# Where attention output is turned token by token: in the feed-forward stage instead of the gradient phase

## The chip, the cores and the metric

The kernel runs on one core of one Trainium2 chip. The metric is the device time of one execution in microseconds (us), and the time of a kernel is the median of several runs. The kernel computes the forward and the backward pass of one transformer block in a single launch.

In the profile PE is the engine that does matrix products and transposes, DVE, ACT and POOL do elementwise work, and SP only issues DMAs. SPq and POOLq rows are DMA issues on the instruction streams of SP and POOL; each stream runs strictly in order, and a DMA whose data or buffer isn't ready holds up everything behind it on that stream.

## The reference

The block is an attention part that runs over 64 segments one after another, with 8 memory tokens carried from segment to segment, and a SwiGLU feed-forward part. All tensors are bf16; S = 2048 tokens, D = 448, 16 heads of 256 (4096 columns, HD), F = 1792.

```python
h  = x + A(layernorm(x))          # A: segments of 32 tokens + 8 memory tokens
h2 = h + B(layernorm(h))          # B: (silu(x @ w_gate) * (x @ w_up)) @ w_down

# A, for each segment s, hcat = concat(mem, xs):
q, k, v = hcat @ Wq, hcat @ Wk, hcat @ Wv
p = softmax(where(mask, q @ k.T * scale, -1e9))
o = (p @ v) @ Wo
mem = o[:8]; out_s = o[8:]

out, vjp = jax.vjp(f, A_x, A_mem0, A_Wq, A_Wk, A_Wv, A_Wo, w_gate, w_up, w_down)
return out, *vjp(grad_out)
```

So ten outputs: the block's output and nine gradients. The gradient of Wo is a product of `p @ v` (called O here, all 4096 columns of it) with the gradient that reaches the attention output, summed over all tokens, and the gradients of Wq, Wk and Wv are products of the normed input with dQ, dK and dV.

## The kernel before

The program has four stages, in this order.

**Forward chain** (`forward_chain`). 64 segments in sequence; four segments make one tile of 128 token rows, t = 0 to 15. For each tile it keeps O in feature-major form, `oA` (128 features by 32 chunks by 128 tokens), and when the fourth segment of the tile is done POOL stores it to the DRAM tensor `OTA[t]`, 1 MB each. The eight memory tokens of each segment go to `OTB`.

**Feed-forward stage** (`ffn_phase`, with buffers that `_FFN` cuts out of the large SBUF tensor `Wall`, whose quarters W[0] to W[3] hold weights). A loop `for i in range(NT - 2)` goes over the tiles. Each iteration handles several tiles at once: the gradient `dz` and the output of tile t, the gate and up products of the next tile n1, the norm of the one after, n2. What it does on the two DMA streams, in program order, with the line that issues it:

- SP: `load(n2)` (L1055, L1057, L1058) loads the rows of `Hh` and of grad_out of tile n2. Its buffer `h_ld` has three slots, and the slot becomes free when `down_ev` (L1149) of tile t-1 has read it. The data is needed by `norm(n2)` (L1063), late in the same iteration.
- POOL: `DH` and `DHb` of tile t-1 (L1179, L1182), `DGP` and `DU` of tile t (L1158, L1161), `doutT` (L1198), the block's output (L1150), `HN` (L1066), `Zt` of tile n1 (L1116). The buffers `dh_t` (of `DH`), `dgp` and `du` have one slot each, so DVE can write the next tile's values only when the store of this one has landed. `z` has two.
- In iteration i = 2 there is also `load_back` of the transposed Wo: four DMA transposes on SP (L1016, L1017) and a memset on POOL (L1018), which overwrites rows that the last of them has written and therefore waits for it.

**Backward chain** (`backward_chain`): the 64 segments in reverse, which store dQ, dK and dV feature-major as `dQA`, `dKA`, `dVA`, in the same form as `OTA`.

**Gradient phase** (`tail_phase`). It has 22 pieces, p = 0 to 21. Pieces 0 to 5 are feed-forward weight gradients. Pieces 6 to 21 are the four quarters (1024 of 4096 columns) each of v, k, q and o, in this order. Each piece is one run of matrix products over all tokens (L1864 and L1877 for v, k and q; L1849 for o) with a 5 MB operand X, which holds tokens in the partitions. There are three X buffers, so X of piece p+2 takes the buffer of piece p-1; `load_phase(p + 2)` is written at the start of piece p. As the stored tensors are feature-major, `seg_x` turns them while loading: 16 DMA transposes on SP (L1804), one for each tile, of 128 by 1024 values (256 KB). The rows of the memory-adjacent tokens come by another way: `seg_b_load` (POOL, L1813), a POOL copy (L1819), PE transposes (L1826). Also on SP in every piece from 5 on are three loads for the last layernorm (L1888 to L1892) and, from 6 on, a store of the result (L1904); in piece 8 there are the loads of the 2 MB operand of the o pieces (L1796 to L1799).

The change touches `_FFN`, the loop of `ffn_phase`, and `seg`, `srcA` and `load_phase` of `tail_phase`.

Of the kernel before, what the change touches and what calls it, by code (L numbers as in the profile page):

```python
# [10 lines left out]
BF16 = mybir.dt.bfloat16  # L11
# [4 lines left out]
P = 128  # L16


class _Prio:

    def __init__(self, tc):
        self.tc = tc
        self.next = -50_000_000
# [242 lines left out]
def run_all(k: _K):  # L266
    nc, tc, ctx = k.nc, k.tc, k.ctx
    S, D, M, H, Dh, HD, F = k.S, k.D, k.M, k.H, k.Dh, k.HD, k.F
    SEG, L, NSEG, NT, KC, DP, MC, DC, FC = k.SEG, k.L, k.NSEG, k.NT, k.KC, k.DP, k.MC, k.DC, k.FC
# [12 lines left out]
    dram = ctx.enter_context(tc.tile_pool(name="dram", bufs=1, space=bass.MemoryType.DRAM))  # L282
# [13 lines left out]
    def ps3(n=3):  # L296
# [32 lines left out]
    Vtok = dram.tile([NSEG, 2, 48, HD // 2], BF16, name="Vtok")  # L329
    OTA = dram.tile([NT, P, MC * P], BF16, name="OTA")  # L330
    OTB = dram.tile([NT, P, MC * SEG], BF16, name="OTB")
    DHb = dram.tile([S, D], BF16, name="DHb")
    dxnTd = dram.tile([NT, P, KC * P], FP32, name="dxnTd")
    memTd = dram.tile([P, KC, NSEG * M], BF16, name="memTd")
    dmemTd = dram.tile([P, KC, NSEG * M], BF16, name="dmemTd")
    memtok = dram.tile([NSEG * M, D], BF16, name="memtok")
    dmemtok = dram.tile([NSEG * M, D], BF16, name="dmemtok")
    dQA = dram.tile([NT, P, MC * P], BF16, name="dQA")
    dKA = dram.tile([NT, P, MC * P], BF16, name="dKA")
    dVA = dram.tile([NT, P, MC * P], BF16, name="dVA")  # L340
    dQB = dram.tile([NT, P, MC * SEG], BF16, name="dQB")
    dKB = dram.tile([NT, P, MC * SEG], BF16, name="dKB")
    dVB = dram.tile([NT, P, MC * SEG], BF16, name="dVB")
    doutTd = dram.tile([NT, P, KC * P], BF16, name="doutTd")
    P_all = dram.tile([NSEG, 64 + L, H // 2 * 64], BF16, name="P_all")
    dr = dict(XN=XN, Hh=Hh, HN=HN, DH=DH, Zt=Zt, DGP=DGP, DU=DU, QtokA=QtokA, KtokA=KtokA, QtokB=QtokB, KtokB=KtokB, Vtok=Vtok,
              OTA=OTA, OTB=OTB, DHb=DHb, dxnT=dxnTd, memT=memTd, dmemT=dmemTd, memtok=memtok, dmemtok=dmemtok, dQA=dQA, dKA=dKA, dVA=dVA, dQB=dQB, dKB=dKB, dVB=dVB, doutT=doutTd, P_all=P_all)
    k.dr = dr

    wts = ExitStack()  # L350
# [3 lines left out]
    W = [k.Wall[:, i * WS:(i + 1) * WS] for i in range(4)]  # L354
    ff = _FFN(k, W)
# [26 lines left out]
    with tc.manual_schedule():  # L382
# [25 lines left out]
        Xs = W[3][:, 0:NT * D].rearrange("p (t d) -> p t d", t=NT)  # L408
# [72 lines left out]
def forward_chain(k: _K, hA, NWIN, Wq_sb, Wk_sb, Wv_sb, Wo_sb, maskr, work, stage, ff, feed):  # L481
# [290 lines left out]
    for s in range(NSEG):  # L772
# [172 lines left out]
        if r == 3:  # L945
            nc.gpsimd.dma_start(out=dr["OTA"][t], in_=T.oA[:].rearrange("p c n -> p (c n)"))
            nc.gpsimd.dma_start(out=dr["OTB"][t], in_=T.oB[:].rearrange("p c n -> p (c n)"))
        late2 = late
# [15 lines left out]
class _FFN:  # L964

    def __init__(self, k, W):
        self.k = k
        P_, F, D, KC, FC = P, k.F, k.D, k.KC, k.FC
        n1 = KC * F
        n2 = FC * D  # L970
        self.Wg = W[0][:, 0:n1].rearrange("p (c f) -> p c f", c=KC)
        self.Wu = W[0][:, n1:2 * n1].rearrange("p (c f) -> p c f", c=KC)
        self.Wd = W[1][:, n1:n1 + n2].rearrange("p (c d) -> p c d", c=FC)
        self.zT = W[1][:, n1 + n2:n1 + n2 + F].rearrange("p (c n) -> p c n", c=FC)
        self.WgT = W[2][:, 0:n2].rearrange("p (c d) -> p c d", c=FC)
        self.WuT = W[2][:, n2:2 * n2].rearrange("p (c d) -> p c d", c=FC)
        self.dgpT = W[2][:, 2 * n2:2 * n2 + F].rearrange("p (c n) -> p c n", c=FC)
        self.duT = W[2][:, 2 * n2 + F:2 * n2 + 2 * F].rearrange("p (c n) -> p c n", c=FC)

    def load_first(self):  # L980
        k, nc = self.k, self.k.nc
        D = k.D
        full = D // P
        rem = D - full * P
        for dst, src, eng in ((self.Wg, k.aps["B_w_gate"], nc.gpsimd), (self.Wu, k.aps["B_w_up"], nc.gpsimd)):
            eng.dma_start(out=dst[:, 0:full, :], in_=src[0:full * P, :].rearrange("(kc p) n -> p kc n", p=P))
            for h in range(2):
                eng.dma_start(out=dst[rem * h:rem * (h + 1), full, :], in_=src[full * P:D, :])
# [21 lines left out]
def load_back(k, v, src, head, c0=0, c1=None):  # L1010
    nc = k.nc
    D, HD = k.D, k.HD
    if head:
        full = D // P
        for kc in range(full):
            nc.sync.dma_start_transpose(out=v[:, kc, :], in_=src[:, kc * P:(kc + 1) * P])  # L1016
        nc.sync.dma_start_transpose(out=v[:, full, :], in_=src[:, D - P:D])  # L1017
        nc.gpsimd.memset(v[0:P - (D - full * P), full, :], 0.0)  # L1018
    else:
        nc.sync.dma_start_transpose(out=v[:, c0:c1, :], in_=src[:, c0 * P:c1 * P])  # L1020


def ffn_phase(k: _K, WT, ff, work, mv2, rstd2, srcs, back):
    nc, tc = k.nc, k.tc
    S, D, F = k.S, k.D, k.F
    NT, KC, DP, FC = k.NT, k.KC, k.DP, k.FC
    ps1, ident, dr = k.ps1, k.ident, k.dr
# [21 lines left out]
    def rows(t):  # L1049
        return slice(t * P, (t + 1) * P)  # L1050

    def load(t):
        o = T[t]
        o.h = work.tile([P, D], BF16, name="h_ld", bufs=3)
        nc.sync.dma_start(out=o.h[:], in_=dr["Hh"][rows(t), :])  # L1055
        o.dout = work.tile([P, DP], BF16, name="dout_ld", bufs=4)
        nc.sync.dma_start(out=o.dout[:, 0:D], in_=GO2[rows(t), :])  # L1057
        nc.sync.dma_start(out=o.dout[:, D:DP], in_=GO2[rows(t), D - rem:D])  # L1058
# [125 lines left out]
    def dh_out(t):  # L1184
# [12 lines left out]
        A(dT[:], pt[:, 0:KC * P])  # L1197
        nc.gpsimd.dma_start(out=dr["doutT"][t], in_=dT[:])  # L1198

    sd = smal.tile([P, NT], FP32, name="sd2")  # L1200

    def rstd(a, b):
# [30 lines left out]
    for i in range(NT - 2):  # L1233
        t, n1, n2 = ORD[i:i + 3]
        if i > 0:
            load(n2)
        if i == 2:
            load_back(k, WT["o"], srcs["o"], True)
        if i == NT - 6:
            next(back)  # L1240
        turn_f(T[t].z, ff.zT, (A, A))
        dz(t)
        if i > 0:
            dh_ln(t - 1)
        down_mm(t)
        if i == 0:
            rstd(NT - 1, NT)
        grads(t)
        if i > 0:
            dh_out(t - 1)  # L1250
        gate(n1)
        down_ev(t)
        norm(n2)
        up(n1)
        if i == NT - 3:
            dout_turn(n1)
            hn_turn(n2)
            gate(n2)
            load_back(k, WT["v"], srcs["v"], False, 0, HC)
            up(n2)  # L1260
            load_back(k, WT["v"], srcs["v"], False, HC, 2 * HC)
            dh_turn(t)
            slope(n1)
            slope(n2)
        else:
            dh_turn(t)
            dout_turn(n1)
            hn_turn(n2)
            slope(n1)
        dh_mm(t)  # L1270
    p, q = ORD[NT - 2:]
# [483 lines left out]
def tail_phase(k: _K, work):  # L1755
    nc, tc = k.nc, k.tc
    S, D, M, HD, F = k.S, k.D, k.M, k.HD, k.F
    SEG, NSEG, NT, KC, MC = k.SEG, k.NSEG, k.NT, k.KC, k.MC
    ps1, ident, identf, dr = k.ps1, k.ident, k.identf, k.dr
# [6 lines left out]
    NKT = NT + NG  # L1766
    FH = F // 2
    NQ = HD // 1024
# [32 lines left out]
    def seg_x(srcA, q, p):  # L1801
        X = k.Wall[:, k.xpos[p] * 512:k.xpos[p] * 512 + NKT * 1024].rearrange("p (t f) -> p t f", t=NKT)
        for t in range(NT):
            nc.sync.dma_start_transpose(out=X[:, t, :].rearrange("n (c p) -> n c p", p=P),  # L1804
                                        in_=srcA[t][:, q * 1024:(q + 1) * 1024])
        return X

    def seg_b_load(srcB, q):
        n = 8 * SEG
        lds = []  # L1810
        for g in range(NG):
            ld = work.tile([P, 4, n], BF16, name="ldb", bufs=4)
            nc.gpsimd.dma_start(out=ld[:], in_=srcB[4 * g:4 * g + 4].rearrange("t p f -> p t f")[:, :, q * n:(q + 1) * n])  # L1813
            lds.append(ld)
        return lds
# [91 lines left out]
    Xs = {}  # L1907
    lds = {}
    lns = {}
    seg = [(w, q) for w in "vkqo" for q in range(NQ)]  # L1910
    srcA = {"v": dr["dVA"], "k": dr["dKA"], "q": dr["dQA"], "o": dr["OTA"]}
    srcB = {"v": dr["dVB"], "k": dr["dKB"], "q": dr["dQB"], "o": dr["OTB"]}
    outs = {"q": OUT[3].rearrange("d h e -> d (h e)"), "k": OUT[4].rearrange("d h e -> d (h e)"),
            "v": OUT[5].rearrange("d h e -> d (h e)"), "o": OUT[6].rearrange("h e d -> (h e) d")}
# [3 lines left out]
    def load_phase(p):  # L1918
        if p >= NP:
            return  # L1920
        if p == 0:
            Xs[p] = k.x_first
        elif p < 6:
            Xs[p] = k.ffn_half(ffn[p], p, 1)
        else:
            Xs[p] = seg_x(srcA[seg[p - 6][0]], seg[p - 6][1], p)

    load_rows(GO_all, GO2, 4)
    yield
# [5 lines left out]
    for p in range(NP):  # L1935
# [23 lines left out]
        if 5 <= p < NP - 1:  # L1959
            if p not in lds:  # L1960
                w, q = seg[p - 5]
# [12 lines left out]
        else:  # L1974
            w, q = seg[p - 6]
# [45 lines left out]
```

## Time and profile before

| what | value |
|---|---|
| median of 3 runs | 2984.47 us |
| lowest, highest | 2972.53, 2985.21 us |
| profiled execution, its own time | 2984.53 us |
| span of the profiled execution | 2982.8 us |
| mean granted PE clock | 0.976 |
| busy over the span: PE, DVE, ACT, POOL | 92%, 52%, 37%, 25% |
| DMA, share of 16 engines: issued by SP, by POOL | 45.0%, 19.7% |
| one iteration of the feed-forward loop, steady | 20.31 us |
| gradient phase, first to last product | 2296.8 to 2976.2 us |

The times are microseconds from the start of the span. A row of the timeline gives the start, the duration, the engine, the line of the kernel, the operation, the output and input tensors by name, and in brackets the idle time before it and what ended it. PE is busy nearly all the time, but its share is an average over four stages: in the steady iterations of the feed-forward loop it has no gap at all, in the chains it has many small ones, and in the gradient phase it has few, which lie close together.

### The profile page before, as it was taken

How to read it: one execution, taken by the hardware profiler on the slowest of the kernel's cores; microseconds unless marked ns; L12 is line 12 of the kernel's file. 1: busy time of each engine (PE TensorE's matmuls, PEld its weight loads, DVE VectorE, ACT ScalarE, POOL GpSimd, SP SyncE). 2: the span in 40 equal slices, each digit the busy share in tenths (PEclk: the TensorE clock that was granted, in tenths of full speed). 3: DMA queues.
4: the chain of work that ended last, by engine and by line, in shares of the span. 5: the costliest groups of instructions: out<-in, count | busy, mean ns of one | idle time of the engine just before them, and what ended most of it. 6: DMA issues, size and time to landing. Idle time of an engine off the chain costs nothing.

```text
span 2982.8 us, 104752 instructions
## 1 busy us (share of the span) xinstructions
PE 2746.4 (92%) x44552; PEld 1524.2 (51%) x44588; DVE 1561.9 (52%) x4196; ACT 1099.0 (37%) x2904; POOL 745.3 (25%) x1388
## 2 busy tenths in 40 slices
PE   2999999999998699998999999999998999999989
PEld 1555555555554355554555555555554554444444
DVE  3666666666665477775666666656663111112211
ACT  1444444444443466553434344334432111111100
POOL 1222222222222122221222222222222233322232
PEclk7999999999999899998999999999999999999999
DMA  9344444444436863376565655655567999999995
GB/s 255 113 126 127 127 126 133 123 127 127 127 122 150 194 164 125 124 207 163 145 162 167 168 152 153 184 148 159 163 174 262 282 219 217 193 197 205 185 205 117
DMA packets 623395, 493.61 MB, mean 165 GB/s; under 512 B 486128, under 2 KB 535648, under 8 KB 613392
## 3 DMA queue, kind: packets, MB, share of 16 engines
q1 hardware_dynamic: 574592, 295.20, 45.0%
q0 software_dynamic: 48336, 191.70, 19.7%
q8 instruction: 352, 5.77, 0.8%
q14 instruction: 115, 0.94, 0.1%
HBM read 137.50 MB, written 221.94 MB: 121 GB/s over the span
## 4 chain that ended last, share of the span: by engine, by line
PE 38%; DVE 9%; DMA 3%; issue 3%; ACT 1%; POOL 1%; SPq 1%; ACTq 0%; DVEq 0%; POOLq 0%
PE psf L1864 12%; PE psf L1364 8%; DVE arena L1327 5%; PE psf L1849 4%; PE psf L1673 3%; PE psf L1336 3%; PE psf L1877 2%; PE psf L1371 2%; ACT arena L1330 1%; PE psh L1699 1%; DVE arena L1659 1%; DVE arena L1653 1%; DVE arena L1656 1%; DVE rsum L1655 1%; PE psh L1826 1%
## 5 line engine op out<-in xcount | busy, mean ns | idle before, releaser
L1864 PE MATMUL psf<-wall,arena 128*128 128x512 bf16 (+1 forms) x1788 | 394.0, 375 | 8.6 <-DMA wall<-dKA 6.5
L508 ACT CAST arena<-psf 128x512 bf16<-128x512 f32 (+2 forms) x560 | 235.7, 452 | 373.2 <-PE psf L545 259.2
L1330 ACT CAST arena<-psf 128x256 bf16<-128x256 f32 (+1 forms) x597 | 233.4, 418 | 306.4 <-PE psf L1336 214.9
L545 PE MATMUL psf<-wall,arena 112*32 112x512 bf16 x5120 | 309.1, 383 | 39.1 <-DMA wall<-in_A_Wk_dram 17.5
L1364 PE MATMUL psf<-wall,arena 128*32 128x448 bf16 x6144 | 334.4, 360 | 7.0 <-DMA wall<-in_A_Wq_dram 5.8
L1864 PEld LDWEIGHTS <-arena 128*128 128x128 bf16 x1824 | 176.7, 98 | 208.0 <-issue 16.9
L1779 DVE CAST arena<-psf 128x512 bf16<-128x512 f32 (+1 forms) x75 | 49.7, 662 | 427.3 <-PE psf L1864 280.3
L505 DVE CAST arena<-psf 128x512 bf16<-128x512 f32 (+2 forms) x432 | 191.8, 469 | 134.9 <-PE psf L545 93.1
L1777 ACT CAST arena<-psf 128x448 bf16<-128x448 f32 (+1 forms) x83 | 46.4, 559 | 490.9 <-PE psf L1864 286.6
L1364 PEld LDWEIGHTS <-arena 128*32 128x32 bf16 x6144 | 154.6, 98 | 123.4 <-issue 16.9
L545 PEld LDWEIGHTS <-arena 112*32 112x32 bf16 x5120 | 126.3, 97 | 170.2 <-issue 36.4
L1327 DVE CAST arena<-psf 128x256 bf16<-128x256 f32 (+1 forms) x339 | 164.7, 486 | 86.4 <-PE psf L1673 43.8
L1849 PE MATMUL psf<-arena,wall 128*128 128x448 bf16 x864 | 172.1, 358 | 18.3 <-DMA wall<-OTA 9.8
L553 PE MATMUL psf<-wall,arena 112*32 112x512 bf16 x2560 | 169.2, 385 | 12.1 <-DMA wall<-in_A_Wv_dram 12.1
L1336 PE MATMUL psf<-wall,arena 128*32 128x512 bf16 x2560 | 157.6, 382 | 1.2 <-DVE arena L1376 1.2
L508 ACT COPY arena<-psh 40x160 bf16<-40x160 bf16 (+2 forms) x320 | 118.9, 399 | 94.6 <-PE psh L657 52.8
L1673 PE MATMUL psf<-arena 40*128 40x40 bf16 x6144 | 147.7, 178 | 6.3 <-issue 3.6
L674 PE MATMUL psf<-wall,arena 128*32 128x224 bf16 x5120 | 146.8, 265 | 0.0
L1724 POOL COPY arena<-arena 128x32 bf16<-128x32 bf16 x63 | 13.2, 210 | 529.7 <-DVE arena L1376 529.7
L1673 PEld LDWEIGHTS <-arena 40*128 40x128 bf16 x6144 | 126.1, 93 | 37.4 <-issue 17.1
L511 POOL COPY arena<-arena 32x512 bf16<-32x512 bf16 x129 | 77.8, 603 | 268.1 <-ACT arena L508 249.9
L1327 DVE COPY arena<-arena 32x512 bf16<-32x512 bf16 x384 | 133.5, 348 | 8.8
(219 smaller groups left out, 4367.9 us busy)
## 6 DMA issues: line engine op xcount, KB each, us to landing
Vtok<-arena SPq DMA_DIRECT2D x128, 192.0 KB
KtokA<-arena SPq DMA_DIRECT2D x64, 256.0 KB
QtokA<-arena SPq DMA_DIRECT2D x64, 256.0 KB
OTA<-arena POOLq DMA_DIRECT2D x16, 1024.0 KB, 4.9
arena<-QtokA SPq DMA_DIRECT2D x128, 128.0 KB
arena<-KtokA SPq DMA_DIRECT2D x128, 128.0 KB
dVA<-arena POOLq DMA_DIRECT2D x16, 1024.0 KB, 5.1
dKA<-arena POOLq DMA_DIRECT2D x16, 1024.0 KB, 7.3
```

What stands on the lines that cost most here:

```text
L505: nc.vector.tensor_copy(out=out, in_=in_)
L508: nc.scalar.copy(out=out, in_=in_)
L545: nc.tensor.matmul(ps[32 * g:32 * g + 32, :], lhsT=stat(kc), rhs=W_sb[0:DB, kc, c0:c0 + HB], start=(kc == 0), stop=(kc == KC - 1))
L553: nc.tensor.matmul(ps[32 * g:32 * g + 32, :].rearrange("t (y d) -> t y d", y=2), lhsT=stat(kc), rhs=wv[:, x, :, half, e, :], start=(kc == ...
L674: nc.tensor.matmul(ps[32 * g:32 * g + 32, 0:2 * DB], lhsT=x, rhs=Wo_sb[:, c, a * 2 * DB:(a + 1) * 2 * DB], start=first, stop=last)
L1327: nc.vector.tensor_copy(out=out, in_=in_)
L1330: nc.scalar.copy(out=out, in_=in_)
L1336: nc.tensor.matmul(ps[32 * g:32 * g + 32, :], lhsT=stat(kc), rhs=WoT_sb[:, kc, c0:c0 + HB], start=(kc == 0), stop=(kc == KC - 1))
L1364: nc.tensor.matmul(pO[32 * g:32 * g + 32, 0:D], lhsT=ch(c), rhs=WT[:, c, :], start=(first and i < 4), stop=(last and i >= MC - 4), skip_gr ...
L1673: nc.tensor.matmul(po[:, n * L:(n + 1) * L], lhsT=lhs[b:b + L, lc:lc + P], rhs=rhs[b:b + L, hh, 0:L], start=True, stop=True)
L1849: nc.tensor.matmul(ps[:, 0:D], lhsT=stat[:, i, c * P:(c + 1) * P], rhs=Y[:, i, 0:D], start=(i == 0), stop=(i == kts - 1))
L1864: nc.tensor.matmul(ps[:, 0:N], lhsT=Hx[:, i, dc * P:(dc + 1) * P], rhs=X[:, i, b * N:(b + 1) * N], start=(i == 0), stop=(i == kts - 1))
```

## The change

O gets a second copy in DRAM, `OTok`, with tokens first. In iterations 1 to 12 of the feed-forward loop, after `load(n2)`, the new function `o_turn` takes the next six (iterations 1 to 4) or five (5 to 12) of the 64 quarter tiles of `OTA`. For each one SP issues the same DMA transpose that `seg_x` issued in the gradient phase, into one of three buffers of 256 KB in free parts of W[0] and W[1], and POOL stores the buffer to `OTok`. The gradient phase loads an o quarter from `OTok` with two plain DMAs of 2 MB (`seg_o`), and the order of pieces 6 to 21 is now v0 v1 v2 v3 k0 k1 o0 k2 k3 o1 q0 q1 o2 q2 q3 o3.

```diff
+    OTok = dram.tile([NT, P, HD], BF16, name="OTok")
...
+        self.ot = [W[0][:, 2 * n1:2 * n1 + 1024], W[0][:, 2 * n1 + 1024:2 * n1 + 2048], W[1][:, n1 + n2 + F:n1 + n2 + F + 1024]]
...
+    quarters = [(t, q) for t in range(NT) for q in range(4)]
+
+    def o_turn(n):
+        for t, q in quarters[:n]:
+            b = ff.ot[len(quarters) % 3]
+            del quarters[0]
+            cols = slice(q * 1024, (q + 1) * 1024)
+            nc.sync.dma_start_transpose(out=b.rearrange("n (c p) -> n c p", p=P), in_=dr["OTA"][t][:, cols])
+            nc.gpsimd.dma_start(out=dr["OTok"][t][:, cols], in_=b)
...
         t, n1, n2 = ORD[i:i + 3]
         if i > 0:
             load(n2)
+        if 0 < i < NT - 3:
+            o_turn(6 if i < 5 else 5)
         if i == 2:
             load_back(k, WT["o"], srcs["o"], True)
...
+    def seg_o(q, p):
+        X = k.Wall[:, k.xpos[p] * 512:k.xpos[p] * 512 + NKT * 1024].rearrange("p (t f) -> p t f", t=NKT)
+        v = dr["OTok"].rearrange("t n f -> n t f")[:, :, q * 1024:(q + 1) * 1024]
+        for a in range(0, NT, NT // 2):
+            nc.sync.dma_start(out=X[:, a:a + NT // 2, :], in_=v[:, a:a + NT // 2, :])
+        return X
...
-    seg = [(w, q) for w in "vkqo" for q in range(NQ)]
-    srcA = {"v": dr["dVA"], "k": dr["dKA"], "q": dr["dQA"], "o": dr["OTA"]}
+    turned = [(w, q) for w in "vkq" for q in range(NQ)]
+    seg = turned[0:6] + [("o", 0)] + turned[6:8] + [("o", 1)] + turned[8:10] + [("o", 2)] + turned[10:12] + [("o", 3)]
+    assert NQ == 4
+    srcA = {"v": dr["dVA"], "k": dr["dKA"], "q": dr["dQA"]}
...
-            Xs[p] = seg_x(srcA[seg[p - 6][0]], seg[p - 6][1], p)
+            w, q = seg[p - 6]
+            Xs[p] = seg_o(q, p) if w == "o" else seg_x(srcA[w], q, p)
```

More of the change, by code (lines that the diff above doesn't have):

```diff
@@ L346, in run_all @@
     dr = dict(XN=XN, Hh=Hh, HN=HN, DH=DH, Zt=Zt, DGP=DGP, DU=DU, QtokA=QtokA, KtokA=KtokA, QtokB=QtokB, KtokB=KtokB, Vtok=Vtok,
-              OTA=OTA, OTB=OTB, DHb=DHb, dxnT=dxnTd, memT=memTd, dmemT=dmemTd, memtok=memtok, dmemtok=dmemtok, dQA=dQA, dKA=dKA, dVA=dVA, dQB=dQB, dKB=dKB, dVB=dVB, doutT=doutTd, P_all=P_all)
+              OTA=OTA, OTB=OTB, OTok=OTok, DHb=DHb, dxnT=dxnTd, memT=memTd, dmemT=dmemTd, memtok=memtok, dmemtok=dmemtok, dQA=dQA, dKA=dKA, dVA=dVA, dQB=dQB, dKB=dKB, dVB=dVB, doutT=doutTd, P_all=P_all)
     k.dr = dr
```

## The prediction

> **What bounds the kernel now.** I read the windows of busy time by stage first, then the chain of waits, then the timelines of SP, POOL and DVE where a wait showed. PE is the bound in both stages that the change touches:
>
> ```profile
> 1100.00:1200.00 100.00, 100.00 (x711) 52.93 (x709) 76.14 (x130) 61.71 (x105) 21.46 (x40) 1.00 0.32 116
> ...
> 2500.00:2600.00 100.00, 99.53 (x590) 49.29 (x597) 21.53 (x41) 11.65 (x17) 30.32 (x40) 1.00 1.07 208
> 2600.00:2700.00 100.00, 92.92 (x540) 45.39 (x547) 20.24 (x39) 12.78 (x16) 25.38 (x33) 0.95 1.11 196
> ```
>
> The columns are the window, its length, busy us of PE, PEld, DVE, ACT and POOL, granted clock, DMA share and GB/s. In the feed-forward loop (first row) PE never rests and DMA is used to a third. In the gradient phase DMA is full and PE mostly hides it; the window at 2600 and the one at 2800 (PE 88.46, clock 0.93) are where it doesn't. The chain shows the first:
>
> ```profile
> 2626.32 3.56 PE psf L1864 x16
> ...
> 2660.76 8.56 DMA wall<-dKA
> 2670.16 11.88 PE psf L1864 x43
> ...
> 2701.66 3.56 PE psf L1864 x16
> ...
> 2734.33 3.56 PE psf L1864 x16
> ```
>
> Rows "x16" open a piece. An undisturbed piece takes 2734.33 - 2701.66 = 32.67 us, so p = 13 (k3) should open at 2658.99 and end at 2691.66; it ends at 2701.66, 10.0 late: 6.7 us of waiting for the turned dKA, and 43 products in 11.88 us where other pieces have 9.44, at a lowered clock. In the same way p = 17 loses 1.8 us, and the o pieces take 142.1 us (2834.10 to 2976.19) where 640 products at 0.189, twelve groups of transposes at 0.45 and four at 0.44 make 128.3: 13.8 lost, most of it while o0 waits for `OTA`. **All that the gradient phase can give back is 10.0 + 1.8 + 13.8 = 25.6 us.**
>
> Why X is late is seen on SP:
>
> ```profile
> 2477.24 29.12 SPq L1804 DMA_TRANSPOSE wall<-dVA  x16
> ...
> 2628.43 33.77 SPq L1804 DMA_TRANSPOSE wall<-dKA  x16
> ...
> 2801.05 38.18 SPq L1804 DMA_TRANSPOSE wall<-OTA  x16
> ```
>
> A turned quarter keeps SP 26 to 38 us, as long as a piece computes; the loads of the o operand at 2534 to 2557 put SP some 20 us behind, and nothing lets it catch up.
>
> **Gradient phase after.** Pieces 6 to 11 are as before; k1 is in time today. Then o0's 4.2 MB go plainly. Plain loads moved 12.0 MB in 75.5% of 46 us in the window 2297 to 2343, 2.9 us for each MB, so 12 us in place of 30. SP comes to k2's transposes at about 2606, not 2628; with 34 us for sixteen they end at 2640, wanted at 2659 with some 7 us of landing: 12 us to spare. k3 can start when k1's buffer is free (2626), follows k2 and ends at 2675, wanted at 2691. After that every second or third piece is plain and X is limited by its buffer (q0: free 2691, done 2723, wanted 2757). The two new DMAs of a plain quarter replace sixteen on SP, so the layernorm loads and L1904's stores behind them come earlier. I take the full 25.6 us back; the bounds are 25.6 and, if other small waits arise, 15.
>
> **The feed-forward loop: direct cost.** PE, DVE and ACT get no new instruction. SP gets 64 transposes, POOL 64 stores of 0.54 us, hidden by its 8.56 us wait in every iteration. The nearest rows for a transpose are those of `Vtok`, 192 KB at a median of 1.29 us, so 1.72 us for 256 KB, and those of L1804, 1.6 to 2.4; for a store of 256 KB 3.0 us to landing alone (`KtokB`) and 4.9 in the full gradient phase. With three buffers the fourth transpose waits for the first store: SP needs about 12 us for six, POOL is held till some 14 us after `load(n2)`, where `DH` is due at 12. That delay is covered, since `dh_t` is written again a whole iteration of 20.31 us later. The next `load(n2)` keeps its place 20 us on. DMA: before, 0.33 x 20.31 = 6.7 us for each iteration; added 6 x (1.7 + 0.7) = 14.4, together 21; with five 18.7. That is full but not over, as shares of up to 1.13 occur. I take zero for the steady iterations; the bounds are 0 and 3 us for each of twelve (below).
>
> **The feed-forward loop: i = 2.** Here the cover is already used up today:
>
> ```profile
> 1045.72 19.09 SPq L1016 DMA_TRANSPOSE wall<-in_A_Wo_dram  x3
> ...
> 1047.30 0.54 POOL L1116 DMA_DIRECT2D Zt<-wall  x1 [1.57 <-DVE wall L1115]
> 1071.78 3.50 POOL L1018 MEMSET wall<- 64x4096 bf16 x1 [23.94 <-DMA wall<-in_A_Wo_dram]
> 1075.23 0.54 POOL L1179 DMA_DIRECT2D DH<-arena  x1
> ...
> 1077.55 0.69 DVE L228 SCALAR_TENSOR_TENSOR arena<-arena,rstd 128x448 f32<-128x448 f32 x1 [1.85 <-DMA DH<-arena]
> ```
>
> POOL's memset waits for Wo's transposes from 1048 to 1072, the `DH` store behind it is 19 us late, and DVE, which rewrites its only buffer, waits 1.85 us. PE didn't feel it. Now six transposes stand ahead of Wo's on SP: three at 1045.7, the others after the first stores (issued behind `Zt` at 1047.8, landed near 1053), so Wo's start at 1057 to 1059, 12 us later. Everything follows: Wo landed at 1084, memset done at 1087.5, `DH` out, L228 at 1090 in place of 1077.5; then `dgp` and `du`, one slot each, wait for `DGP` and `DU` issued behind `DH` (0.7 us more). L1105, which empties the gate's PSUM banks, starts at about 1094.8, was 1081.76. PE can fill six banks; today it starts the second pair of up at 1084.15, 1.2 us after the first two are emptied. It stops there until 1096: 11.8 us, and 2.5 us more at a lowered clock, as after the stall at 2670 (11.88 - 9.44). **Cost 14 us.** Bounds: 3, if Wo's transposes run faster while POOL, being held, stores nothing beside them (they moved 290 GB/s when alone at 1060 to 1062, 4.2 MB in 14.5 us against the 26 seen); 19, if the six take 16 us beside stores. I stay near the upper half, because the last three stores fall beside Wo's start, as `Zt` did, which then took 10.5 us to land and not 2.7.
>
> **Sum**: 2984.53 - 25.6 + 14 = 2973. The profiled execution is at the median (2984.47); the lowest run, 2972.53, shows that the kernel itself moves by 12 us, so 0.5% (15 us) is about what can be told from no change.
>
> **Rivals.**
>
> (a) *Little is lost at i = 2.* The lower bound: 2984.5 - 25.6 + 3 = 2962. For it: Wo alone is fast. Against it: three 256 KB stores beside its start. 2957 to 2967.
>
> (b) *DMA becomes the bound of the feed-forward loop.* Traffic for each iteration was 2.34 MB and becomes 5.5, then 5.0 MB, or 270 and 245 GB/s; the gradient phase, full of transposes, moves 195 to 243. At 243, 5.5 MB take 22.6 us and 5.0 MB 20.6: 2.3 us over in each of four, 0.3 in eight, 12 us in all; at 220, 4.7 and 2.4 over, 38 in all. It would show as `load(n2)` landing after L1063 wants it. It decides as soon as transposes and stores of one iteration need more than 20.31 us. Time: 2985 to 3011, 2998 in the middle, slower than before. Against it: only 29% of the bytes are turned here, against 65% in the gradient phase, and transposes alone moved 290 GB/s, plain loads 333. [...]
>
> (c) *Stalls remain in the gradient phase*, for the loads of the memory rows (L1819 waited 21.3 us in seven cases for `OTB`) or at k2: 15 us of gain in place of 25.6, 2984.
>
> (d) *The plain quarter takes as long as the turned one*, because the phase's mixture, not the transpose, sets the rate. Then all 25.6 us stay and 14 come on top: 2998. Against it: 333 GB/s in pieces 0 and 1 against 195 to 243 later. [...]
>
> **Chances.** Forecast 0.45 (2965 to 2982); (a) 0.15; (b) 0.25; (c) 0.10; (d) 0.05. Faster than 2969.5: (a) and a quarter of the forecast, 0.27. Slower than 2999.4: half of (b) and part of (d), 0.14. Within 0.5%: 0.59. The range takes (a) and the lower half of (b), and leaves out some 0.15: 2957 to 3002; the forecast's own is 2965 to 2982.
>
> **What would show it.** Right: no wait of L1864 or L1849 for X after p = 12; k2's transposes start near 2606 less the shift; one PE gap near 1084 to 1096 with the Wo memset ending near 1087; the other iterations at 20.31 us. Wrong: iterations of 21 us or more, waits of L1063 for `Hh` or of POOL's stores beyond `DH`'s next use (b); a memset that ends before 1080 (a); waits for `OTok` (d).

## The result, and the profile after

The changed kernel takes 2997.15 us (median of 8 runs, 2984.71 to 3005.04) against 2983.99 us (8 runs, 2971.84 to 2992.52) for the kernel before on the same chip: a ratio of 1.0062, 95% interval 1.0035 to 1.0088. By that ratio it is slower by some 18 us (10 to 26), by the two medians by 13, where 2973 and a gain of 11 were forecast.

The profiled executions, by stage. "Loop" is from the first product of the gate (L1089 before, L1091 after) to the last transpose of `dh_out` (L1189, L1191). The first wait in it, of the gate's products for DVE (L1105) at the loop's start, came out between 11 and 21 us in kernels whose code is the same there, so it is a row of its own; "loop, net" is the number that all experiments are compared by.

| us | before | after | difference |
|---|---|---|---|
| own time of the execution | 2984.53 | 2998.80 | +14.3 |
| to the first gate product | 978.6 | 971.7 | -6.9 |
| first wait in the loop | 20.9 | 18.7 | -2.2 |
| loop, net | 344.4 | 375.2 | +30.8 |
| backward chain, to the first product of the gradient phase | 952.9 | 955.0 | +2.1 |
| gradient phase, first to last product of L1849's kind | 679.0 | 671.4 | -7.6 |

So the loss lies in the feed-forward loop, and the gain in the gradient phase is smaller than forecast. The windows of busy time of the changed kernel (window, length, busy us of PE, PEld, DVE, ACT and POOL, granted clock, DMA share, GB/s):

```profile
1080.00:1100.00 20.00, 4.95 (x22) 2.08 (x23) 5.33 (x7) 1.78 (x4) 9.33 (x12) 0.55 1.00 263
1100.00:1200.00 100.00, 99.69 (x710) 53.02 (x707) 76.16 (x128) 60.53 (x103) 35.16 (x65) 1.00 0.99 244
1200.00:1300.00 100.00, 97.30 (x691) 51.24 (x691) 72.51 (x126) 59.29 (x101) 32.40 (x60) 1.00 0.98 238
...
2600.00:2700.00 100.00, 88.18 (x524) 44.77 (x527) 20.34 (x40) 10.17 (x15) 26.40 (x37) 0.93 1.12 230
2800.00:2900.00 100.00, 99.63 (x593) 51.17 (x599) 21.39 (x41) 11.35 (x17) 33.55 (x45) 1.00 1.09 233
```

In the loop PE stands until 1095 and loses little afterwards, while DMA went from 116 to 244 GB/s. In the gradient phase the weak window at 2800 is healed, and the one at 2600 is worse than before. The timeline of the changed kernel shows the stop, on SP, POOL, DVE and PE in turn:

```profile
1036.88 22.97 SPq L1209 DMA_TRANSPOSE wall<-OTA  x6
1059.90 19.78 SPq L1018 DMA_TRANSPOSE wall<-in_A_Wo_dram  x3
...
1046.27 0.54 POOL L1210 DMA_DIRECT2D OTok<-wall  x1 [5.61 <-DMA wall<-OTA]
1053.73 0.54 POOL L1210 DMA_DIRECT2D OTok<-wall  x1 [6.91 <-DMA wall<-OTA]
...
1086.47 3.50 POOL L1020 MEMSET wall<- 64x4096 bf16 x1 [22.80 <-DMA wall<-in_A_Wo_dram]
1089.92 0.54 POOL L1181 DMA_DIRECT2D DH<-arena  x1
...
1093.88 0.69 DVE L228 SCALAR_TENSOR_TENSOR arena<-arena,rstd 128x448 f32<-128x448 f32 x1 [27.10 <-DMA DH<-arena]
...
1095.05 0.61 PE L1191 MATMUL psh<-ident,arena 128*128 128x128 bf16 x4 [24.47 <-DVE arena L1041]
```

It is the chain that the prediction described: six transposes, then Wo's, then the memset, `DH`, L228. But the six hold SP for 22.97 us where 12 were forecast: 10.1 us of it SP waits for stores, as its waits from 1036 to 1061 show.

```profile
SPq L1209 <- DMA OTok<-wall: 10.1, 2, 8.9
```

PE stops not at the second pair of up but earlier, at the four transposes of `dh_out` (L1191), which stand before them in its order and need what L228 gives. It stands 24.47 us where 11.8 were forecast; which of the two misses made the difference is worked out below.

In the gradient phase (waits of PE: total, times, longest; then SP's timeline):

```profile
PE psf L1885 <- DMA wall<-dKA: 11.4, 4, 4.5
```

```profile
2540.07 34.17 SPq L1818 DMA_TRANSPOSE wall<-dKA  x16
...
2599.05 32.19 SPq L1818 DMA_TRANSPOSE wall<-dKA  x16
2633.73 1.00 SPq L1826 DMA_DIRECT2D wall<-OTok  x2
```

There is no wait for X behind p = 12 any more, as forecast. But k1, which the prediction called in time, now waits: its transposes start 278.5 us into the phase (2599.05 - 2320.6), in the kernel before 265.0 (2561.82 - 2296.8), as the five turned quarters ahead of them took 159.7 us of SP and not 142.8.

### The profile page after: what moved, and what is told of

The parts are those of the page before. It is cut to its first block, busy times and chain, and to the rows that moved or that the text cites. A ratio compares the mean times of both kernels' runs of the same rounds, so it can differ in the third digit from the quotient of the medians.

```text
span 2997.0 us, 104830 instructions
## 1 busy us (share of the span) xinstructions
PE 2746.4 (92%) x44552; PEld 1523.9 (51%) x44588; DVE 1561.9 (52%) x4196; ACT 1099.9 (37%) x2904; POOL 782.5 (26%) x1452
## 3 DMA queue, kind: packets, MB, share of 16 engines
q0 software_dynamic: 53456, 208.48, 21.5%
## 4 chain that ended last, share of the span: by engine, by line
PE 38%; DVE 9%; DMA 3%; issue 3%; ACT 1%; POOL 1%; SPq 0%; ACTq 0%; DVEq 0%; POOLq 0%
PE psf L1885 11%; PE psf L1378 8%; DVE arena L1341 5%; PE psf L1870 4%; PE psf L1687 3%; PE psf L1350 3%; PE psf L1898 2%; PE psf L1385 2%; ACT arena L1344 1%; PE psh L1713 1%; DVE arena L1673 1%; DVE arena L1667 1%; DVE arena L1670 1%; DVE rsum L1669 1%; PE psh L1847 1%
## 5 line engine op out<-in xcount | busy, mean ns | idle before, releaser
L1885 PE MATMUL psf<-wall,arena 128*128 128x512 bf16 (+1 forms) x1788 | 393.1, 374 | 13.5 <-DMA wall<-dKA 11.4
L1738 POOL COPY arena<-arena 128x32 bf16<-128x32 bf16 x63 | 13.4, 212 | 534.5 <-DVE arena L1390 534.5
L1687 PEld LDWEIGHTS <-arena 40*128 40x128 bf16 x6144 | 125.6, 93 | 37.1 <-issue 16.7
L1044 ACT COPY wall<-psh 128x896 bf16<-128x896 bf16 (+1 forms) x142 | 105.1, 833 | 104.4 <-PE psh L1191 55.4
```

What stands on the lines that cost most here:

```text
L1687: nc.tensor.matmul(po[:, n * L:(n + 1) * L], lhsT=lhs[b:b + L, lc:lc + P], rhs=rhs[b:b + L, hh, 0:L], start=True, stop=True)
L1885: nc.tensor.matmul(ps[:, 0:N], lhsT=Hx[:, i, dc * P:(dc + 1) * P], rhs=X[:, i, b * N:(b + 1) * N], start=(i == 0), stop=(i == kts - 1))
```

## The experiments

Each ratio is against runs of the kernel before on the same chip. Line numbers are those of each kernel and differ by a few. The "loop, net" of a run comes from its one profile. The theories on trial were: the loss is the one event at i = 2 (A); six transposes and stores through three buffers don't fit into an iteration (B, F); the gradient phase gives what was counted (C), or its new order brings new waits (D); `OTok`'s place in DRAM (E); transposes and stores slow each other on the DMA engines in every iteration (G, the mixture); POOL, in order, stands at stores that wait for transposes, with `DH` behind them (H, the hold or tie).

### The two halves: e2_ffn_only, e3_tail_only

e2 has the turning and the stores in the loop, and the gradient phase of before. e3 has the new gradient phase alone:

```diff
-        if 0 < i < NT - 3:
-            o_turn(6 if i < 5 else 5)
...
-        v = dr["OTok"].rearrange("t n f -> n t f")[...]
+        v = dr["OTA"].rearrange("t n f -> n t f")[...]
```

> The quarters are turned in the feed-forward loop as in the change, but the gradient phase loads o turned from OTA in the old order, as before the change; the copy in OTok is not read. Theory A: the loop costs 28 to 31 us whatever the gradient phase does, so 3013 (ratio 1.010), and the gradient phase takes 679 us as before. Rival: part of the loss belongs to the gradient phase or to the chains and was only seen in one profiled execution: below 3003.

> Nothing is turned in the feed-forward loop; the gradient phase has the new order and loads the o quarters plainly, but from OTA, so the gradient of Wo is computed from unturned values. Theory C (plain quarters give back what the prediction counted, and the stall at k1 in the changed kernel was a matter of that execution): 2984 less 20 to 26, 2958 to 2964 (ratio 0.992), no wait for X in any piece. Theory D (the new order or the plain loads themselves bring new waits, for X at k1 or for the memory rows): 2970 to 2980, with waits of PE for dKA or of POOL's copy for its loads.

Measured: e2 1.0124 (1.0068 to 1.0179), loop net 375.3; e3 0.9924 (0.9890 to 0.9957), loop net 344.3. The loop half costs some 37 us (0.0124 of 2970.5), the gradient half gives 23, and each interval is 10 to 17 us wide to either side. The profiles give a steadier size of the second: the gradient phase took 667.5 to 701.5 us in six profiles with the old order (before, e2, g3, g4, h1, k1; mean 683.9) and 653.5 to 681.3 in eleven with the new one (after, e1, e3, e4, g1, h2, h4, k2, k3, k4, l1; mean 669.3). The gain is near 15 us, with a standard error of some 6; waits for `dKA`, all of them at k1, remain in ten of the eleven (2.6 to 15.6 us). So e3's time agrees with C, and its profile has the waits at k1 that D spoke of (9.3 us).

### The event at i = 2, and where OTok lies: e1_skip2, e4_last, h2_late_memset

```diff
 e1:
-            o_turn(6 if i < 5 else 5)
+            o_turn({1: 6, 2: 0, 11: 5, 12: 5}.get(i, 6))
 e4: OTok is declared as the last DRAM tensor
 h2:
-        nc.gpsimd.memset(v[0:P - (D - full * P), full, :], 0.0)
...
+        if i == 4:
+            nc.gpsimd.memset(WT["o"][0:P - (k.D - k.D // P * P), k.D // P, :], 0.0)
```

> Turning is left out of iteration 2 only; iterations 1 and 3 to 10 turn six quarters, 11 and 12 five. Theory A (the loss in the feed-forward loop is the held POOL stream behind the Wo memset, whose transposes stood behind six turned quarters): the PE gap of 24.5 us before dh_out in iteration 3 is gone, the memset ends as early after Wo's issue as before the change, and the time falls by 24 to 27 us against the changed kernel, to about 2972 (ratio 0.996 to the kernel before). Theory B (the loop as a whole is short of DMA, and the gap is only where it shows first): the lost time comes back as smaller waits in later iterations, now with six quarters in most of them; 2985 to 3000.

> The changed kernel with OTok declared last, so that every other DRAM tensor lies where it lay before the change. Theory E (OTok moved dVA, dKA and the others to addresses at which the turned loads of pieces 6 to 10 run slower, 159.7 us of issue for five quarters against 142.8): the five take 141 to 146 us again, k1 is in time, and the time falls by about 13 us to 2984. Theory C (chance): no difference beyond the spread, 2990 to 3003.

> The changed kernel as it is, with POOL's memset behind Wo's transposes written two iterations later (i = 4), where Wo landed long ago. This asks whether the chain of the prediction for i = 2 (Wo late, memset late, DH late, L228 late, PE stops) goes through the memset. If it does: the gap of 24 us at the DH products of i = 2 is gone, the loop less its first stall takes 348 to 355 us (375 in the changed kernel), ratio 0.996 to 0.999. If the stores to OTok hold POOL just as long, since their transposes run beside Wo's: a gap of 8 us or more stays at i = 2 or comes in i = 3, the loop takes 362 or more, ratio 1.002 to 1.006.

Measured: e1 1.0077 (1.0035 to 1.0119), loop net 388.9; e4 1.0060 (1.0033 to 1.0087), 375.2; h2 1.0120 (1.0069 to 1.0171), 393.9. Where nothing is turned in i = 2, the single stop is gone, and more is lost in small pieces. The waits of e1 in the loop, POOL's, DVE's and SP's, and the landing of `Zt` at 1100 to 1250 (2.7 us before):

```profile
POOL OTok L1210 <- DMA wall<-OTA: 179.4, 49, 10.1
...
DVE arena L228 <- DMA DH<-arena: 51.7, 10, 8.0
...
SPq L1209 <- DMA OTok<-wall: 118.9, 31, 11.6
```

```profile
Zt<-wall POOLq DMA_DIRECT2D x6, 448.0 KB, 10.2
```

SP waits for stores, POOL for transposes, and L228 in ten iterations for `DH`, which stands behind both. From i = 3 on six transposes hold SP 18 to 24 us, about as long as an iteration (20.31) or longer. So A falls as the whole account.

E isn't settled. e4's ratio is that of the changed kernel, where E expected 13 us less. But its one profile shows what E said: the five turned quarters ahead of k1 took SP 139.7 us, PE didn't wait for `dKA`, and the gradient phase took 653.5 us, 25.5 less than before the change. In the kernel before the five took 142.8 us; in the eighteen other profiles, all of kernels that declare `OTok` ahead of `dQA`, `dKA` and `dVA`, 152.6 to 162.5. So the place of `OTok` may well slow the turned loads of that phase. One profile of each kernel can't show it, and why e4's time didn't follow stays open.

h2 shows that the memset isn't the lock: without it POOL's stores of i = 2 and 3 waited for transposes just as long (25.76 us in one case), and Wo's four, no longer shielded by a standing POOL, took 37.1 us of SP and not 24.4.

### One part alone: g3_turn_only, g4_store_only

The order of e1 and the old gradient phase; g3 leaves the stores out, g4 the transposes (its buffers are cleared once).

```diff
 g3:
-            nc.gpsimd.dma_start(out=dr["OTok"][t][:, cols], in_=b)
 g4:
-            nc.sync.dma_start_transpose(out=b.rearrange("n (c p) -> n c p", p=P), in_=dr["OTA"][t][:, cols])
```

> Turning alone, in the schedule of e1_skip2, into three buffers; the stores to OTok are left out and the gradient phase loads o turned from OTA in the old order. Theories F, G and H all let the loop fall, by how much is what tells: if transposes alone fill the loop's DMA (G, transposes as the dear part) it stays above 380; if they need the stores beside them to hurt (F, H, or G by the mixture) it is 365 to 370.

> The stores to OTok alone, in the schedule of e1_skip2, with the transposes left out (three buffers are cleared once and stored), and the gradient phase as before the change. Expected by F and H 365 to 368: 0.54 us of issue each and no wait. By G with stores as the dear part: above 375.

Measured: g3 1.0021 (0.9992 to 1.0051), loop net 344.9; g4 0.9990 (0.9967 to 1.0014), 346.7. Each alone costs 0.5 and 2.3 us. (The expectations of the g runs count the first wait too; so counted, the loop took 356.9 and 360.7 us.) Six transposes alone hold SP 9.4 to 13.1 us, near the prediction's 1.72 us each, in the longest case:

```profile
1094.75 13.05 SPq L1209 DMA_TRANSPOSE wall<-OTA  x6
```

A store alone lands in 4.0 us. In this schedule it is the two together that cost 44.5 (e1).

### More buffers, later stores: g1_seven, g2_deferred

g1 has seven buffers and no turning in i = 2; g2 also issues the stores, on POOL, one iteration later.

```diff
+    ff.ot += [arena.view(68608 + 2048 * j, [P, 1024], BF16) for j in range(4)]
...
-            b = ff.ot[len(quarters) % 3]
+            b = ff.ot[len(quarters) % len(ff.ot)]
```

> As e1_skip2 (no turning in iteration 2, six quarters in iterations 3 to 10), but with seven buffers, four of them in a free part of the arena; for that the first loads of the backward chain move from iteration 10 to 13. The loop, from the first gate product to the last dh_out, took 365 us before the change and 402 in e1_skip2. Theory F (the chain of three buffers sets the pace: the fourth transpose waits for the first store to land): with seven no transpose waits for a store of its own iteration, and the loop falls to 365 to 375. Theory G (the 16 DMA engines can't move six turned quarters and their stores beside the loop's own traffic in 20.31 us): it stays at 395 or more. Theory H (POOL, which waits in order for each transpose to land before it can issue the loop's own stores): something between, since the wait for the sixth transpose remains; 380 to 395.

> As g1_seven, but POOL stores each group of quarters one iteration after it was turned, so that it never waits for a transpose. Theory H: DH goes out when DVE has it, no wait of L228 for DH, loop at 365 to 370, and with the gradient phase's gain the kernel is faster than before, ratio 0.992 to 0.995. Theory G: the loop stays above 385, waits of DVE for DH or of L1065 for Hh remain, ratio 1.002 or more.

Measured: g1 1.0039 (1.0009 to 1.0068), loop net 367.0; g2 1.0008 (0.9975 to 1.0041). Buffers are a part of it, 22 us against e1 (388.9), but 23 us over the kernel before are left. Counted as in its expectation, with the first wait, g1's loop took 386.5 us, which is what H said, and not F. For g2, what H expected (0.992 to 0.995) lies outside the interval, and what G expected (1.002 or more) lies inside it in part. The intervals of g1 and g2 overlap, so that later stores help isn't shown, and g2's one profile, of its slowest execution (3002.42 us), isn't compared here. So the tie itself was taken away next.

### Without a tie: h1, k1, k2, k4

h1 runs both parts side by side with no wait between them (transposes into buffers that nobody reads, stores from cleared ones); k1 is h1 with the memset at i = 4; k2 and k4 are g1 and e1, with their ties, and the memset at i = 4.

```diff
 h1:
             nc.sync.dma_start_transpose(out=b.rearrange("n (c p) -> n c p", p=P), in_=dr["OTA"][t][:, cols])
+            nc.gpsimd.dma_start(out=dr["OTok"][t][:, cols], in_=ff.clear[len(quarters) % 4])
```

> Both kinds of DMA in the loop, with no wait between them: the 64 transposes go into three buffers that nobody reads, the 64 stores to OTok take their values from four other buffers that were cleared once, so POOL waits for no transpose. The numbers for each iteration are those of the kernel that skips i = 2, and the gradient phase is the old one, so the time is to be read from the loop and against 1. Left out of the computation: nothing that an output needs (OTok isn't read). In profiles, from the first gate product to the last DH product less the stall at the loop's start, the kernel before takes 344 us, turning alone 345, storing alone 347, both tied together 367 to 389. Theory of the mixture (transposes and stores slow each other on the DMA engines, whatever waits for what): 365 us or more, six transposes hold SP 17 us or more, the Zt store takes 8 us or more, ratio 1.006 to 1.013. Theory of the hold (POOL, in order, stands at stores that wait for transposes, and DH stands behind them): 345 to 350 us, Zt 3 to 5 us, ratio 0.999 to 1.003.

> The kernel with turning and storing side by side without a wait between them, and Wo's memset written at i = 4 and not behind Wo's transposes, so POOL isn't held in i = 2 and has no backlog of stores to let go. The gradient phase is the old one. Theory of the transient: transposes of i = 3 to 5 take 12 to 19 us for six (30 and 41 with the backlog), the loop less its first stall takes 345 to 352 us (372 with the backlog), ratio 0.999 to 1.004. Theory of the mixture in every iteration: 362 us or more, ratio 1.006 or more.

> The kernel with seven buffers, where POOL stores each quarter in order behind its transpose, with Wo's memset at i = 4. Theory of the transient alone: 345 to 352 us (367 with the memset in i = 2), ratio 0.991 to 0.997. Theory of the tie (POOL's DH stands behind stores that wait for transposes, in every iteration): 358 to 367 us, L228 still waits 10 us or more for DH in all, ratio 0.998 to 1.003.

> The kernel with three buffers and no turning in i = 2, with Wo's memset at i = 4. Theory of the transient alone: 345 to 355 us (389 with the memset in i = 2), ratio 0.991 to 0.998. Theory of the chain through three buffers (a fourth transpose waits for the first store, so six take 18 to 24 us of SP, more than an iteration of 20.31, and POOL waits with them): 372 us or more, ratio 1.003 to 1.008.

| | ratio | loop, net | Wo's four on SP | six transposes on SP, 1110 to 1240 |
|---|---|---|---|---|
| h1 | 1.0127 (1.0065 to 1.0189) | 372.0 | 25.0 | 41.1, then 12.8 to 18.4 |
| k1 | 1.0085 (1.0057 to 1.0114) | 367.3 | 44.3 | 13.4 to 17.9 |
| k2 | 1.0036 (1.0001 to 1.0072) | 377.1 | 39.3 | 18 to 24 |
| k4 | 1.0117 (1.0073 to 1.0160) | 404.4 | 49.4 | 20.6 to 25.9 |

By ratio h1 speaks for the mixture, but the profile doesn't: its loss lies in a few iterations. h1's timeline (POOL's memset, SP's transposes):

```profile
1064.40 3.50 POOL L1021 MEMSET wall<- 64x4096 bf16 x1 [26.68 <-DMA wall<-in_A_Wo_dram]
...
1083.67 30.44 SPq L1213 DMA_TRANSPOSE wall<-OTA  x6
...
1118.82 41.11 SPq L1213 DMA_TRANSPOSE wall<-OTA  x6
...
1161.56 13.92 SPq L1213 DMA_TRANSPOSE wall<-OTA  x6
```

POOL, let go at 1068, issues 19 stores within 17 us; the transposes crawl, and the rows of `Hh` behind them are 13.3 us late. From 1160 on, with the same traffic, six take 12 to 18 us. k1, without the hold, has one loss: the last of Wo's transposes (the six behind it took 29.7 us too, but nothing waited for them), and behind it `Hh` (SP's timeline, DVE's wait), and after it PE is full (windows):

```profile
1052.53 25.32 SPq L1020 DMA_TRANSPOSE wall<-in_A_Wo_dram  x1
```

```profile
DVE arena L1065 <- DMA arena<-Hh: 20.6, 1, 20.6
```

```profile
1030.00:1100.00 70.00, 49.91 (x350) 27.08 (x349) 38.67 (x65) 31.75 (x54) 16.57 (x31) 0.85 1.19 182
1100.00:1200.00 100.00, 100.00 (x714) 53.06 (x712) 75.01 (x128) 58.89 (x101) 37.45 (x66) 1.00 1.15 282
```

PE is busy 100 of 100 us while 282 GB/s move: the full traffic of turning and storing fits. So my expectation that 362 us or more would mean a loss in every iteration was too coarse; of k1's 22.9 us, 20.1 are the one wait of PE at L1132. With the tie (k4, one row of SP's timeline for each of three iterations) it doesn't fit:

```profile
1116.23 20.57 SPq L1208 DMA_TRANSPOSE wall<-OTA  x6
1140.37 23.23 SPq L1208 DMA_TRANSPOSE wall<-OTA  x6
1167.24 25.89 SPq L1208 DMA_TRANSPOSE wall<-OTA  x6
```

With seven buffers (k2) the tie still costs: L228 waits 30.2 us for `DH` in seven iterations, and the loop, 377.1, is longer than either theory said. In all three kernels with the tie the late memset made the loop longer (h2 against the changed kernel, k2 against g1, k4 against e1: 10 to 19 us), as Wo's four took 37 to 49 us, and 24.4 to 28.7 where a standing POOL had kept stores away from them.

### Versions without both causes: h4, k3, l1, and half of the work: h3, l2

In h4, SP issues the stores, one iteration after the transposes and ahead of the next ones; seven buffers. k3 is h4 with the memset at i = 4. In l1, four quarters are turned in i = 0, none in 1 and 2, six in 3 to 12, so that nothing added runs beside Wo. h3 is the changed kernel with o0 and o1 alone (three in an iteration), l2 is l1 with o0 and o1 alone.

```diff
 h4, l1:
+        for out, in_ in due:
+            nc.sync.dma_start(out=out, in_=in_)
+        due.clear()
...
-            nc.gpsimd.dma_start(out=dr["OTok"][t][:, cols], in_=b)
+            due.append((dr["OTok"][t][:, cols], b))
...
 l1:
+        o_turn({0: 4, 1: 0, 2: 0, 13: 0}.get(i, 6))
 h3, l2:
-    quarters = [(t, q) for t in range(NT) for q in range(4)]
+    quarters = [(t, q) for t in range(NT) for q in range(2)]
```

> All 64 quarters are turned in the loop (none in i = 2) into seven buffers, and stored to OTok one iteration later by SP, ahead of the next transposes, so that POOL issues no store to OTok and SP waits for nothing that isn't long done; the new order of the gradient phase. Theory of the hold: the loop less its first stall takes 345 to 350 us, ratio 0.991 to 0.994. Theory of the mixture: stores and transposes still run beside each other and beside Zt, DH, DGP and DU: 362 us or more, Zt 8 us or more, ratio 0.997 to 1.003.

> The kernel in which SP stores the quarters one iteration after turning them, with Wo's memset at i = 4. POOL has neither a hold nor a tie left, so by both theories the loop loses nothing: 344 to 348 us, no wait of L228 for DH over 2 us, and the gradient phase's gain stays whole: ratio 0.990 to 0.995. If the mixture on the DMA engines costs by itself: 352 us or more.

> Half of the work: only the quarters o0 and o1 are turned in the loop (two transposes in i = 1, none in i = 2, three in each of i = 3 to 12), and o2 and o3 are turned in the gradient phase as before, with the order v0 v1 v2 v3 k0 k1 o0 k2 k3 q0 q1 o1 q2 q3 o2 o3. Theory that the loop's cost grows with what has to pass beside its own traffic, and that POOL's slack of 8 us in each iteration covers a short hold: the loop less its first stall takes 346 to 352 us, the gradient phase gives back 15 to 22 us, ratio 0.992 to 0.996. Theory that every transpose beside a store costs the same: half of 31 us in the loop, 358 to 362, ratio 0.996 to 1.001.

> SP stores the quarters one iteration after turning them; Wo's memset is where it was, in i = 2; four quarters are turned in i = 0, none in i = 1 and 2, six in each of i = 3 to 12, so that no added DMA runs beside Wo's transposes. If the loss has these two causes (stores tied to transposes on POOL, and neighbours that stretch Wo), Wo takes 23 to 26 us, the loop less its first stall 344 to 349 us (344 before, 375 in the changed kernel), and the gradient phase keeps its gain: ratio 0.990 to 0.995. If the mixture costs in every iteration: 355 us or more, ratio 0.996 or more.

> The same with o0 and o1 alone (two quarters in i = 0, three in each of i = 3 to 12), o2 and o3 turned in the gradient phase, in the order v0 v1 v2 v3 k0 k1 o0 k2 k3 q0 q1 o1 q2 q3 o2 o3. By the two causes: 344 to 346 us in the loop, a gradient phase at most 5 us longer than with four plain quarters, ratio 0.991 to 0.997. If the mixture costs in every iteration, this one loses half as much as l1_clear_wo and is the faster of the two by 0.2% or more.

| | ratio | loop, net | gradient phase |
|---|---|---|---|
| h4 | 0.9983 (0.9946 to 1.0019) | 350.7 | 674.8 |
| k3 | 0.9998 (0.9971 to 1.0026) | 355.5 | 674.4 |
| l1 | 0.9989 (0.9967 to 1.0011) | 344.4 | 672.5 |
| h3 | 0.9961 (0.9923 to 0.9999) | 344.6 | 653.6 |
| l2 | 0.9952 (0.9925 to 0.9980) | 343.8 | 665.5 |

l1 turns and stores everything and its loop is as long as before, to the tenth. Its windows, and Wo and the first two groups on SP's timeline:

```profile
1030.00:1100.00 70.00, 70.00 (x506) 37.35 (x505) 54.96 (x92) 44.45 (x77) 18.84 (x30) 1.00 1.08 261
1100.00:1200.00 100.00, 100.00 (x714) 53.06 (x712) 76.14 (x130) 60.20 (x104) 21.55 (x40) 1.00 1.03 268
```

```profile
1034.79 17.19 SPq L1019 DMA_TRANSPOSE wall<-in_A_Wo_dram  x3
1052.08 4.34 SPq L1020 DMA_TRANSPOSE wall<-in_A_Wo_dram  x1
...
1100.65 6.67 SPq L1215 DMA_TRANSPOSE arena<-OTA  x4
1107.37 3.70 SPq L1215 DMA_TRANSPOSE wall<-OTA  x2
```

h4 loses 6 us (L228 waits 5.2 for `DH`) and k3 11 (Wo's four take 36.7 us, 23.9 in h4, and `Hh` is 11.0 late), both at i = 2 and 3. Both miss what was expected, h4's loop barely (350 at most) and k3's by 7 us: with POOL free, its own stores stretch Wo. l1's loop is as expected, its ratio isn't.

That settles the loop: the loss came from the tie and from Wo's neighbours, not from the amount of traffic alone. The tie needs the amount to hurt, though: h3 has it still, through three buffers, and with three quarters in an iteration it loses nothing (344.6). One thing is not separated: a store on SP also goes through another DMA queue than one on POOL (at 1100 to 1250 the queue hardware_dynamic moved 25.33 MB and software_dynamic 16.17 in h4, with the stores on SP, against 12.72 and 24.37 in g1, with the stores on POOL). k1 shows that stores from POOL cost nothing in the steady iterations when nothing ties them; g2, which kept them on POOL an iteration later, has no profile that can be compared. The time isn't settled: l1's gradient phase waited 15.6 us for `dKA`, and its ratio shows 3 us of gain, where the mean gradient phase would give 15 and e3, with the same loop and phase in its profile, measured 23. What sets k1's wait, the place of `OTok` or chance, stays open. l2 is the version that is clearly faster than the kernel before: 14 us (0.0048 of 2969; h3's interval ends at 0.9999). In its profile `dKA` is waited for 2.1 us, in h3's 0.4; whether half of the work helps k1, or these two executions were lucky, wasn't tried.

## Why the prediction was wrong

- **Gradient phase, -25.6.** The direction and place held: no wait for X behind p = 12, waits for `OTok` none, k3 and the o pieces in time. The size was too large: near -15 by seventeen profiles. The step that failed there is "k1 is in time today": the loads of the o operand still stand on SP ahead of k1, and the five turned quarters before it took 159.7 us in the changed kernel and not 142.8, so that the wait of p = 13 came back at p = 11, with 11.4 us. Whether `OTok`'s place in DRAM lengthened them (e4) stays open. The measured size is the prediction's lower bound, 15, and its reason, other small waits, is the right one.
- **Steady iterations, 0.** In the changed kernel itself it nearly held. From one L1191 to the next an iteration takes 20.31 us, and behind the stop and the iteration after it five are longer, by 4.4 us in all, as five transposes, 13.0 to 20.0 us of SP, just fit. The forecast rested on 12 us for six transposes, which is true of transposes alone (9.4 to 13.1). Tied to stores through POOL they took 18 to 24 in e1, from i = 3 on, and stopped PE there for up to 6.9 us in an iteration.
- **i = 2, +14.** This is the step that failed, and in it the term "SP needs about 12 us for six": they held SP 22.97. The forecast had the first store landed near 1053, 7 us after the first transpose was issued. Instead POOL could issue that store only 9.4 us after the transpose (1036.88 to 1046.27), it took 8.4 us to land, and only then could the fourth transpose start. To hold the later links against the forecast, 8.9 us are added to the times of the changed kernel, whose loop ran that much earlier (`dh_out` of i = 2 at 1050.11, before at 1059.02): Wo started at 1068.8 and not at 1057 to 1059, the memset ended at 1098.9 and not at 1087.5, L228 ran at 1102.8 and not at 1090. So the chain was right link by link, and 11 to 13 us late from its first one on. A second step was wrong, the place where PE stops. In the kernel before, the transposes of `dh_out` (L1189) come ahead of the second pair of up, 1.8 us after L228:

```profile
1079.33 0.39 PE L1189 MATMUL psh<-ident,arena 128*128 128x128 bf16 x4
```

So PE stood from 1079.5 to 1104.0 and not from 1084 to 1096. This by itself hardly changes the length, as PE also goes on right behind L228: with the forecast's L228 at 1090 it would have stood 11.7 us, near the 11.8. So the 12.7 us over the forecast are the late start behind the six transposes, not the place. The loop as a whole lost 30.8: 24.6 in this iteration, 1.4 in the next, whose first six products took 2.45 us and not 1.30, at a granted clock of 0.51 (1095 to 1098), and the 4.4 above.

- **The sum.** -15 + 31 is +16, where +18 was measured and -11.6 forecast. Of the 28 us between, 17 are the loop and 11 the gradient phase.
- **Rival (b)**, DMA as the bound of the loop, gave the measured time (2998), but not for its reason. 5.5 MB in 20.31 us did pass, at 268 to 282 GB/s, with PE full (l1, k1), above the 243 that I had taken as a ceiling. SP's transfers did slow POOL's: `Zt`, a store of POOL, landed in 2.7 us before, in 4.4 with SP's transposes alone added (g3) and in 10.2 with transposes and stores (e1). But for the time it mattered very much behind what a store stood: with the same buffers and quarters the loop took 367.0 us with the stores on POOL, each behind its transpose (g1), and 350.7 with the stores on SP an iteration later (h4).
- **Rivals (a), (c), (d).** (a) fell: the memset ended at 1098.9 on the clock of the kernel before, and PE stood for 24.47 us. (c) was right in part, at k1 and not at the memory rows (3.5 us). (d) fell: a plain quarter held SP 1.0 us in three cases and 4.5 in the fourth (L1826), and PE waited for none.

## What to carry to other kernels

A transfer that waits for another one, written into a stream that has other duties, wasn't hidden here by that stream's idle time: what stood behind it waited as well (in e1 POOL waited 179.4 us for transposes, and L228 51.7 us for the `DH` behind them). Issue the second half of such a pair a whole iteration later, on a stream where its data is long there (the loop took 350.7 us in h4, 367.0 in g1), and keep large transposes that something waits for free of neighbours (Wo's four held SP 21.5 us in l1, 49.4 in k4). Fewer such pairs in an iteration can be enough (344.6 in h3). When a late value is followed to PE, look for the first instruction in PE's program order that needs it, not for the one that runs dry in today's profile. And before two profiles are compared by the clock, line them up on a row that both have.

## What the hardware showed that I had not expected

- DMA transposes and stores slowed each other far more than their bytes say, and not evenly: a store of 256 KB landed in 4.0 us without transposes (g4) and in 7.2 beside them (k1), six transposes of 256 KB took 9.4 to 13.1 us alone, 12 to 18 beside stores of the same size, and 30 and 41 us beside a backlog of stores let go at once; Wo's four took 21 to 29 us when POOL stood still, and 37 to 49 when it stored. During the group of 41 us the DMA share was 1.05 to 1.24 with only 128 to 222 GB/s moved, less than the 268 that l1 moves at 1.03.
- Five turned quarters of the gradient phase, with the same code, took SP 139.7 to 162.5 us in twenty profiles, which is a part of what decides whether k1 waits, and not all of it (k4 waits 8.7 us behind 153.4, l2 2.1 behind 156.0). The two shortest, 139.7 and 142.8, are of the two kernels in which `OTok` doesn't lie ahead of `dQA`, `dKA` and `dVA`; the others begin at 152.6.
